# Issuing a small transfer from GpSimd instead of ScalarE, more unread products, and a second PSUM bank in the third segment's end

## The chip, the cores and the metric

The kernel runs on 1 core of one Trainium2 chip. The metric is the time of one execution on the device in microseconds (us). The kernel before has a median of 779.33 us over 3 runs (775.82 to 816.84).

## The reference, cut to what matters

The output is a gated mix of two layers over the same 2048 x 448 input `u`: a long convolution (S4D) and an attention with a memory of the earlier segments (infini-attention, 16 heads of width 28, 4 segments of 512 rows).

```python
# the convolution: a kernel K of 2048 taps for each of 448 channels
P = exp((A * dt)[:, :, None] * pos)              # 448 x 256 states x 2048
K = 2 * einsum("dn,dnl->dl", C, P).real
y = irfft(rfft(K, 4096) * rfft(u.T, 4096))[:, :2048].T + u * D_skip
# the attention, for each segment s in turn
p      = softmax(qs @ ks.T * scale + mask)       # 512 x 512 for each head
a_dot  = p @ vs
a_mem  = (phi(qs) @ M) / (phi(qs) @ z + 1e-6)
o      = g * a_mem + (1 - g) * a_dot             # g = sigmoid(beta), one for each head
M, z   = M + phi(ks).T @ vs, z + sum(phi(ks))
a      = concat(o) @ wo
# the mix, gated for each row
out    = gate * y + (1 - gate) * a
```

## The kernel before, in words

**Two halves.** The first half, up to about 421 us of the span, builds the taps K, the projections q, k and v, the transform of `u` and the segments' memories; nothing in it is touched. The function `second_half` (L1310) writes out the rest: the softmax attention, the second half of the convolution, and the outputs.

**Units and rounds.** The attention is cut into 16 units; unit i is segment `s = i // 4` and group of heads `hg = i % 4` (4 heads). Each unit has 6 rounds r. A round issues one `pair` (L1339): products of scores into the PSUM tile `ps_w` (`weigh`, L1069), which ScalarE turns by exp into `PT`, and products into `ps_mx` (`maxima`, L1021), for the row maxima of unit i+2, which VectorE reduces to `mx`. `peak` (L1335) is a piece of the maxima of unit i+1. GpSimd zeroes the upper triangle of `PT` (`affine_select`, L1099) and issues the small transfers of the maxima (`qu<-mn`, L1062). The products of `PT` with V go to `ps_pv` (`values`, L1106) in the next unit's first three rounds; ScalarE copies the result to `pvs`. Row 28 of each head's 32 rows in `pvs` is the softmax denominator, since V has a column of ones. Units 1 to 12 also carry the convolution's pieces (`cv`): products into `ps_c`, copies by ScalarE (`ks`, `bs`), products of VectorE (`pr`).

**Unread products.** Where a round has nothing else for TensorE, `turn_over` (L1347) issues products of the constant `wz` (128 x 512, bf16) into `ps_pv`; nobody reads them. In unit 0 it stands in every round, and twice more ahead of a `peak`.

**The end of a segment.** In round 2 of units 4, 8 and 12 the generator `seg_end(s)` (L1223) is started for segment s = 0, 1, 2 and is then stepped once a round (more often where the table `STEPS`, L1469, says so). It does, a step at a time: `norm` (L1163), which loads the denominators as a 128 x 64 tile `dn` (a transfer from SBUF to SBUF of 32 KB, issued by ScalarE through `k.adma`, L1167), inverts them on VectorE (`inverse`, L1127: reciprocal, hi and lo part), writes them to eight rows `r8` with two transfers issued by ScalarE (`r<-rs`, L1138), and then for each hg spreads them by one product with `sel` into PSUM and scales `pvs` in place (a `scalar_tensor_tensor`, and for s > 0 a `tensor_tensor` that adds the memory's part `am`); `recall` of the next segment (L1146), the same for the memory's denominators `dm`; the skip term (`skip`, `scaled`: `u` times the gate on ScalarE, times D on GpSimd, L1194); and four tiles of the out projection, each with two halves of products (`wo`) into a PSUM tile of tag "m", and `store` (L1196), which adds the skip term on VectorE and sends the tile to `TB`.

**PSUM** in this half: tags "m" and "pv" have one bank each, "mx", "w" and "c" one tile of two banks each. So a second product into "m" waits until VectorE or ScalarE has read the first one. In segment 2's `norm` the odd hg already take half of "c", which the convolution no longer needs.

**Order.** TensorE, ScalarE and VectorE execute in the order in which the code is written (L1481, L1491, L1530). `k.pin` keeps a transfer or an operation at its place on its engine. Transfers from SyncE, `k.dma` and `k.ldma`, take their place on its queue. The functions as they stand before the change:

Of the kernel before, what the change touches and what calls it, by code (L numbers as in the profile page):

```python
# [983 lines left out]
def attend(nc, k, ap):  # L984
# [28 lines left out]

    STEPS = [(b, hp) for b in range(3) for hp in range(2)]
    MSTEPS = [(b, 1 - hp) for b, hp in STEPS]

# [129 lines left out]
    def recall(s):  # L1146

        dn = ap.tile([128, 64], F32, tag="dm", name="dm", bufs=1)
        k.ldma(dn, k.DM[s - 1].rearrange("j h (i f) -> (j h i) f", f=64))
        yield  # L1150
        am[s] = ap.tile([128, 4, SEG], F32, tag="am", name="am", bufs=1)
        k.ldma(am[s], k.AM[:, :, s - 1].rearrange("h p q -> p h q"))
        yield
        v.tensor_scalar(dn, dn, 1e-6, None, ALU.add)
        yield from inverse(dn, 32, r8)
        yield
        for hg in range(4):
            pb = k.ps("m")
            k.mm(pb, k.sel[32:40], r8[32:40, hg], start=True, stop=True)
            v.scalar_tensor_tensor(am[s][:, hg], am[s][:, hg], k.gh[:, hg : hg + 1], pb, ALU.mult, ALU.mult)  # L1160
            yield

    def norm(s):  # L1163

        pvs = pvss[s]
        dn = ap.tile([128, 64], F32, tag="dn", name="dn", bufs=1)
        k.pin(k.adma(  # L1167
            dn,
            pvs.rearrange("(j e) h q -> e j (h q)", e=32)[28].rearrange("j (i f) -> j i f", f=64),
        ))  # L1170
        yield
        yield from inverse(dn, 0, r8)
        yield
        for hg in range(4):
            o = pvs[:, hg]
            pb = k.ps("c")[:, 0] if s == 2 and hg % 2 else k.ps("m")
            k.mm(pb, k.sel[0:8], r8[0:8, hg], start=True, stop=True)
            v.scalar_tensor_tensor(o, o, k.omg[:, hg : hg + 1], pb, ALU.mult, ALU.mult)
            if s > 0:
                v.tensor_tensor(o, o, am[s][:, hg], ALU.add)  # L1180
            yield

    def skip(s, t):

        i = 4 * s + t
        xt = ap.tile([128, D], F32, tag="xt", name="xt", bufs=4)
        k.ldma(xt, k.u[128 * i : 128 * i + 128])
        return xt
# [32 lines left out]
    old = []  # L1221

    def seg_end(s):  # L1223
        xts = [skip(s, t) for t in range(4)]
        sums, memory = norm(s), recall(s + 1)
        recalled = old.pop() if old else iter(())
        old.append(memory)
        next(sums)
        k.scaling = s > 0
        yield  # L1230
        for t in range(4):
            next(recalled, None)
            if t > 1:
                next(sums)
            k.scaling = s > 0 and t < 3
            yield
        for t in range(0, 4, 2):
            scaled(s, t, xts[t])
            scaled(s, t + 1, xts[t + 1])
            k.scaling = t == 2  # L1240
            yield
        next(memory)
        for hg in range(4):
            next(sums)
            k.scaling = hg < 3
            yield
        for t in range(4):
            if t < 3:
                next(memory)
            po = k.ps("m")  # L1250
            out_mm(s, t, po[:, :D], range(2))
            half.append(s)
            yield "po"
            half.pop()
            out_mm(s, t, po[:, :D], range(2, 4))
            store(s, t, po[:, :D], xts[t])
            yield "po"
        if s == 2:
            for _ in memory:
                yield  # L1260
# [49 lines left out]
def second_half(nc, k, ap, tp, fp, fin):  # L1310
# [13 lines left out]
    def step(g):  # L1324
        return next(g, none) is not none
# [9 lines left out]
    def peak(g):  # L1335
        step(g)
        step(g)
# [9 lines left out]
    def turn_over(n):  # L1347
        pt = k.ps("pv")
        for _ in range(n):
            k.mm(pt, wz[:, :128], wz, start=True, stop=True)  # L1350
# [42 lines left out]
    for i in range(16):  # L1393
# [5 lines left out]
        for r in range(6):  # L1399
# [4 lines left out]
            if r < 2:  # L1404
                if r == 1 and k.half:
                    step(ends[0])
                peak(behind)
            if i == 0 and r in (0, 2):
                turn_over(2)
                peak(behind)  # L1410
            k.spread = r in (1, 2)
            if i > 0 and r < 3:
                step(vals)
                busy = True
                if i % 4 == 0:
                    for t in ((0,), (1,), (2, 3))[r]:
                        k.load_v(i // 4, t)
                if r == 2 and i % 4 == 0:
                    ends.append(k.seg_end(i // 4 - 1))
            for _ in range(STEPS.get((i, r), 2 if i == 14 else 1)):  # L1420
                x = next(ends[0], none) if ends else none
                if x is none:
                    ends = ends[1:]
                busy = busy or x == "po"
            k.catch_up()
            if (i, r) in DIVIDE:
                if k.half:
# [38 lines left out]


SKIPS = ((2, 0), (2, 4), (2, 5), (3, 0), (3, 1), (3, 2))
STEPS = {(13, 2): 2, (13, 3): 3, (13, 4): 2, (13, 5): 2}  # L1469
DIVIDE = {(14, 5): 0, (15, 2): 1, (15, 4): 2}  # L1470


# [296 lines left out]
```

## Time and profile before

| what | value |
|---|---|
| median of 3 runs | 779.33 us |
| the profiled execution's own time | 781.14 us |
| its span, first to last instruction | 779.4 us |
| mean granted clock of TensorE | 0.967 |
| TensorE busy, of the span | 682.8 us (88%) |
| TensorE busy between 421 us and the end (358.4 us) | 323.2 us |
| VectorE, ScalarE, GpSimd busy there | 206.4, 146.8, 74.1 us |

The profile page gives one execution. A timeline row has the start in us, the busy time, the engine, the line, the operation, out<-in and a count; `[3.41 <-ACT PT L1485]` says that the engine sat idle for 3.41 us before it, and whose result came last. Nearly every operation of the engines has the line of a helper (L1485, L1531), so groups go by the names of tiles. ACTq and SPq are the queues on which ScalarE and SyncE issue transfers. A row of the table by stretches has the stretch, its length, the busy time (and instructions) of PE, PEld, DVE, ACT and POOL, the granted clock, the DMA engines' busy share and GB/s.

### The profile page before, as it was taken

To read this page: it belongs to the slowest core of one execution; us is meant where nothing else is said; L and a number is where in the kernel's file an instruction comes from. 1 tells how busy PE (TensorE), PEld (TensorE's weight loads), DVE (VectorE), ACT (ScalarE), POOL (GpSimd) and SP (SyncE) were. 2 spreads that over 40 slices of the span, in tenths; PEclk is the share of its full clock that TensorE was granted. 3 is DMA by queue.
4 is the path that set the end of the run, shared out by engine and by line. 5 is a ranking of instruction groups with operands and counts; after the bars stand their busy time and mean duration, and the time that the engine had idled before them with its cause. 6 is when DMAs were issued, how large, how long until landed. Compare 5 with 4: busy or idle time off the path is not lost.

```text
span 779.4 us, 19822 instructions
## 1 busy us (share of the span) xinstructions
PE 682.8 (88%) x8289; PEld 372.7 (48%) x8289; DVE 562.5 (72%) x758; ACT 502.9 (65%) x621; POOL 158.2 (20%) x193
## 2 busy tenths in 40 slices
PE   1685998999988998889999999898999789969997
PEld 1362555666555665557654444343444333434433
DVE  8989679878999788888874345565746575684486
ACT  4877689889999989988986425564535453451220
POOL 5405300110111101110020002242411231141110
PEclk9998999999999999999999989998999899998899
DMA  9428774234563345733357797998767876655786
GB/s 240 130 74 246 235 247 134 64 107 163 162 209 110 108 138 164 226 128 104 129 198 250 286 327 245 324 341 311 256 233 234 277 247 213 227 189 208 175 267 185
DMA packets 91742, 158.00 MB, mean 203 GB/s; under 512 B 22366, under 2 KB 59734, under 8 KB 91654
## 3 DMA queue, kind: packets, MB, share of 16 engines
q1 hardware_dynamic: 85722, 153.55, 60.0%
q10 hardware_dynamic: 5052, 2.33, 1.2%
q8 instruction: 65, 1.06, 0.6%
q0 software_dynamic: 880, 0.87, 0.3%
q14 instruction: 23, 0.19, 0.1%
HBM read 88.51 MB, written 60.24 MB: 191 GB/s over the span
## 4 chain that ended last, share of the span: by engine, by line
PE 54%; ACT 18%; DVE 14%; DMA 7%; issue 5%; SPq 1%; POOL 1%; ACTq 0%; DVEq 0%; POOLq 0%
PE ps_m L1531 22%; PE ps_c L1531 9%; ACT cs L1485 6%; PE ps_w L1531 6%; PE ps_pv L1531 5%; PE ps_mx L1531 5%; PE ps_arg L1531 4%; PE ps_k L1531 4%; ACT EY L1485 2%; DVE pr L1485 2%; DMA ku<-KD 2%; DVE mx L1485 2%; DVE pvs L1485 1%; DMA WD<-wsp 1%; DVE xl L906 1%
## 5 line engine op out<-in xcount | busy, mean ns | idle before, releaser
L1485 DVE TENSOR_REDUCE mx<-ps_mx 128x2 f32<-128x1024 f32 (+3 forms) x128 | 102.5, 822 | 98.7 <-PE ps_mx L1531 95.6
L1485 ACT ACTIVATE PT<-ps_w 128x1024 f32<-128x1024 f32 (+1 forms) x96 | 84.6, 881 | 132.2 <-PE ps_w L1531 120.3
L366 POOL TENSOR_TENSOR EX<-EX,cab 128x1024 f32<-128x1024 f32 x28 | 53.5, 1914 | 288.2 <-ACT EX L1485 266.4
L1531 PE MATMUL ps_w<-qu,ku 32*128 32x512 f32 (+3 forms) x768 | 90.8, 354 | 10.0 <-ACT PT L1485 9.9
L1485 ACT ACTIVATE cs<-ps_arg 128x1024 f32<-128x1024 f32 x97 | 94.5, 1024 | 3.5 <-DVE Y L414 2.4
L1531 PEld LDWEIGHTS ps_w<-qu,ku 32*128 32x128 f32 x768 | 60.2, 194 | 74.1 <-ACT PT L1485 40.1
L1099 POOL TENSOR_SCALAR_AFFINE_SELECT PT<-PT 128x256 f32<-128x256 f32 (+1 forms) x96 | 47.0, 489 | 229.0 <-ACT PT L1485 226.7
L1531 PE MATMUL ps_m<-xh,w 112*128 112x512 f32 x256 | 91.3, 409 | 1.1 <-DMA w<-WD 1.1
L409 DVE TENSOR_TENSOR X<-EX,cs 128x1024 f32<-128x1024 f32 x56 | 69.4, 1239 | 12.7 <-ACT cs L1485 11.8
L1531 PE MATMUL ps_k<-Y,X 128*32 128x64 f32 x3584 | 64.1, 225 | 14.4 <-DVE Y L414 14.4
L1531 PEld LDWEIGHTS ps_k<-Y,X 128*32 128x32 f32 x3584 | 54.9, 113 | 40.3 <-DVE Y L414 23.2
L413 DVE TENSOR_TENSOR Y<-EY,cs 128x1024 f32<-128x1024 f32 x56 | 70.2, 1253 | 0.0
L1485 ACT ACTIVATE cs<-cs 128x1024 f32<-128x1024 f32 x56 | 59.2, 1057 | 1.3
L1531 PEld LDWEIGHTS ps_m<-xh,w 112*128 112x128 f32 x256 | 48.0, 188 | 20.8 <-issue 7.8
L1485 ACT ACTIVATE EY<-ps_arg 128x1024 f32<-128x1024 f32 x52 | 51.3, 1036 | 4.2 <-PE ps_arg L1531 4.0
L1531 PE MATMUL ps_arg<-ct,lh 64*128 64x512 bf16 x224 | 46.0, 384 | 7.1 <-ACT EY L1485 4.8
L1531 PE MATMUL ps_m<-xl,w 112*128 112x512 f32 x128 | 50.3, 393 | 0.0
L1531 PEld LDWEIGHTS <-lh 64*128 64x128 bf16 x392 | 20.1, 94 | 59.0 <-issue 46.7
L1531 PE MATMUL ps_mx<-ku,qu 32*128 32x512 f32 (+3 forms) x256 | 45.2, 384 | 0.3 <-DMA ku<-KD 0.3
L1531 PE MATMUL ps_pv<-PT,V 128*32 128x128 f32 (+3 forms) x512 | 44.0, 441 | 0.0
L1531 PE MATMUL ps_m<-wo,pvs 128*128 128x448 f32 x96 | 42.4, 572 | 1.4 <-ACT mn L1485 1.1
L415 DVE SCALAR_TENSOR_TENSOR Y<-EY,cs 128x512 f32<-128x512 f32 x56 | 40.1, 716 | 3.8 <-ACT cs L1485 2.6
(219 smaller groups left out, 1292.2 us busy)
## 6 DMA issues: line engine op xcount, KB each, us to landing
w<-WD SPq DMA_DIRECT2D x32, 448.0 KB
qu<-QD SPq DMA_DIRECT2D x16, 512.0 KB
ku<-KD SPq DMA_DIRECT2D x16, 512.0 KB
GU<-gs SPq DMA_DIRECT2D x32, 224.0 KB
GK<-gs SPq DMA_DIRECT2D x8, 896.0 KB
gk<-GK SPq DMA_DIRECT2D x16, 448.0 KB
gu<-GU SPq DMA_DIRECT2D x16, 448.0 KB
ks<-ks SPq DMA_DIRECT2D x32, 224.0 KB
```

The costliest lines, as they stand in the source:

```text
L366: nc.gpsimd.tensor_tensor(o, o, cab, ALU.mult)
L409: v.tensor_tensor(X, ex, t[:, :, 0], ALU.mult)
L413: v.tensor_tensor(Y[:, :, :, :32], lo, y[:, :, :, ::-1], ALU.mult)
L415: v.scalar_tensor_tensor(Y[:, 1, :, 32:], ey[:, :, 32:], -1.0, y[:, 1], ALU.mult, ALU.mult)
L906: v.tensor_tensor(xl[:, :, ts_], pv, xh[:, :, ts_], ALU.subtract)
L1099: nc.gpsimd.affine_select(sl, sl, pat, ALU.is_ge, 0.0, base=0, channel_multiplier=-1)
L1485: x = op(*args, **kw)
L1531: tc.keep_in_program_order(nc.tensor.matmul(*args, **kw))
```

## The change

It has four parts. (1) `norm` issues the transfer `dn<-pvs` from GpSimd instead of ScalarE, for all three segments. (2) Unit 0 gets four unread products ahead of the peak of round 0, and four instead of two behind it, six more in all. (3) In the end of segment 2 the skip term's four products move forward to the steps t = 3 and the next, so that the generator has one step less, and `STEPS` gives up its second step in round 2 and its third in round 3 of unit 13: the scalings are then hg 0 in round 2, hg 1 and 2 in round 3, hg 3 in round 4, together with the first half of the first tile. The odd tiles of segment 2's out projection and the odd products of `recall(3)` take half of "c" instead of "m". (4) Two reorderings in the code: the loads of `u` come after the first step of `norm`, and the loads of V's tiles 2 and 3 after the step of the segment's end. On SyncE's queue the second moves nothing.

```diff
--- before.py
+++ after.py
@@ -1155,7 +1155,7 @@
         yield from inverse(dn, 32, r8)
         yield
         for hg in range(4):
-            pb = k.ps("m")
+            pb = k.ps("c")[:, 0] if s == 3 and hg % 2 else k.ps("m")
             k.mm(pb, k.sel[32:40], r8[32:40, hg], start=True, stop=True)
             v.scalar_tensor_tensor(am[s][:, hg], am[s][:, hg], k.gh[:, hg : hg + 1], pb, ALU.mult, ALU.mult)
             yield
@@ -1164,7 +1164,7 @@
 
         pvs = pvss[s]
         dn = ap.tile([128, 64], F32, tag="dn", name="dn", bufs=1)
-        k.pin(k.adma(
+        k.pin(k.pdma(
             dn,
             pvs.rearrange("(j e) h q -> e j (h q)", e=32)[28].rearrange("j (i f) -> j i f", f=64),
         ))
@@ -1221,20 +1221,23 @@
     old = []
 
     def seg_end(s):
-        xts = [skip(s, t) for t in range(4)]
         sums, memory = norm(s), recall(s + 1)
         recalled = old.pop() if old else iter(())
         old.append(memory)
         next(sums)
+        xts = [skip(s, t) for t in range(4)]
         k.scaling = s > 0
         yield
         for t in range(4):
             next(recalled, None)
             if t > 1:
                 next(sums)
+            if s == 2 and t == 3:
+                scaled(s, 0, xts[0])
+                scaled(s, 1, xts[1])
             k.scaling = s > 0 and t < 3
             yield
-        for t in range(0, 4, 2):
+        for t in range(2 if s == 2 else 0, 4, 2):
             scaled(s, t, xts[t])
             scaled(s, t + 1, xts[t + 1])
             k.scaling = t == 2
@@ -1247,7 +1250,7 @@
         for t in range(4):
             if t < 3:
                 next(memory)
-            po = k.ps("m")
+            po = k.ps("c")[:, 0] if s == 2 and t % 2 else k.ps("m")
             out_mm(s, t, po[:, :D], range(2))
             half.append(s)
             yield "po"
@@ -1404,17 +1407,18 @@
             if r < 2:
                 if r == 1 and k.half:
                     step(ends[0])
+                if i + r == 0:
+                    turn_over(4)
                 peak(behind)
             if i == 0 and r in (0, 2):
-                turn_over(2)
+                turn_over(4 - r)
                 peak(behind)
             k.spread = r in (1, 2)
             if i > 0 and r < 3:
                 step(vals)
                 busy = True
-                if i % 4 == 0:
-                    for t in ((0,), (1,), (2, 3))[r]:
-                        k.load_v(i // 4, t)
+                if i % 4 == 0 and r < 2:
+                    k.load_v(i // 4, r)
                 if r == 2 and i % 4 == 0:
                     ends.append(k.seg_end(i // 4 - 1))
             for _ in range(STEPS.get((i, r), 2 if i == 14 else 1)):
@@ -1422,6 +1426,9 @@
                 if x is none:
                     ends = ends[1:]
                 busy = busy or x == "po"
+            if i > 0 and i % 4 == 0 and r == 2:
+                for t in (2, 3):
+                    k.load_v(i // 4, t)
             k.catch_up()
             if (i, r) in DIVIDE:
                 if k.half:
@@ -1466,7 +1473,7 @@
 
 
 SKIPS = ((2, 0), (2, 4), (2, 5), (3, 0), (3, 1), (3, 2))
-STEPS = {(13, 2): 2, (13, 3): 3, (13, 4): 2, (13, 5): 2}
+STEPS = {(13, 3): 2, (13, 4): 2, (13, 5): 2}
 DIVIDE = {(14, 5): 0, (15, 2): 1, (15, 4): 2}
```

The first place is GpSimd in round 2 of unit 4, where the denominators of segment 0 are loaded. The names: `PT` is the exponential, `qu<-mn` the small transfer of the maxima, `dn<-pvs` the moved one. A piece of the difference:

```order
 L1099 AFFINE_SELECT PT<-PT 128x2x128 x2
 L1062 DMA qu<-mn 4x4x128
-L1099 AFFINE_SELECT PT<-PT 128x2x128 x2
+L1099 AFFINE_SELECT PT<-PT 128x2x128
+L1167 DMA dn<-pvs 128x1x64
+L1099 AFFINE_SELECT PT<-PT 128x2x128
 L1099 AFFINE_SELECT PT<-PT 128x2x256 x2
 L1099 AFFINE_SELECT PT<-PT 128x2x128 x2
```

The transfer now stands between two selects on `PT`; the second of them is behind it on GpSimd, the exponential on ScalarE no longer is.

The second place is ScalarE in the same round, before the change. `pvs<-ps_pv` is the copy with the denominators, `PT<-ps_w` the exponentials that TensorE's scores wait for, `mn` and `bs` copies of the maxima and of the convolution:

```order
L1485 ACTIVATE ks<-ps_c 128x896
L1485 ACTIVATE PT<-ps_w 128x2x512
L1485 ACTIVATE pvs<-ps_pv 128x512
L1167 DMA dn<-pvs 128x1x64
L1485 ACTIVATE PT<-ps_w 128x2x512
L1485 ACTIVATE PT<-ps_w 128x2x256 x2
L1485 ACTIVATE bs<-ps_c 128x896
```

After the change the row of the transfer is gone, and the exponential stands directly behind the copy; at the two later segments likewise.

The third place is TensorE in units 13 and 14, at the third segment's out projection. `ps_m<-wo,pvs` are a tile's products (4 for a whole tile, 2 for half of it), `ps_m<-ident,mx` the transposition of the maxima, which takes the same bank "m". Before:

```order
L1531 MATMUL ps_m<-wo,pvs 128x448 x4
L1531 MATMUL ps_w<-qu,ku 128x512 x6
L1531 MATMUL ps_pv<-PT,V 32x512 x4
L1531 MATMUL ps_m<-wo,pvs 128x448 x4
L1531 MATMUL ps_w<-qu,ku 128x512 x6
L1534 MATMUL ps_m<-ident,mx 16x128
L1531 MATMUL ps_pv<-PT,V 32x384 x4
L1531 MATMUL ps_m<-wo,pvs 128x448 x4
```

The same place after the change, where the helpers' lines are 7 higher:

```order
L1538 MATMUL ps_m<-wo,pvs 128x448 x2
L1538 MATMUL ps_c<-wo,pvs 128x448 x2
L1538 MATMUL ps_w<-qu,ku 128x512 x6
L1538 MATMUL ps_pv<-PT,V 32x512 x4
L1538 MATMUL ps_c<-wo,pvs 128x448 x2
L1538 MATMUL ps_m<-wo,pvs 128x448 x2
L1538 MATMUL ps_w<-qu,ku 128x512 x6
L1538 MATMUL ps_m<-wo,pvs 128x448 x2
L1541 MATMUL ps_m<-ident,mx 16x128
L1538 MATMUL ps_pv<-PT,V 32x384 x4
L1538 MATMUL ps_c<-wo,pvs 128x448 x4
```

The tiles now alternate between the two banks and are cut half a tile later against the rounds; the transposition stands directly behind a tile's last products on the same bank.

## The prediction, made before the changed kernel ran

> **What bounds the kernel now.** I read the shares of the page first, then the table by stretches for the second half of the span, where the change lies.
>
> ```profile
> PE 682.8 (88%) x8289; PEld 372.7 (48%) x8289; DVE 562.5 (72%) x758; ACT 502.9 (65%) x621; POOL 158.2 (20%) x193
> ```
> ```profile
> 460.00:465.00 5.00, 4.07 (x35) 1.67 (x38) 2.27 (x3) 0.74 (x1) 0.40 (x1) 0.61 1.02 393
> 470.00:480.00 10.00, 9.49 (x118) 4.10 (x116) 4.31 (x7) 4.70 (x7) 3.10 (x6) 0.93 0.63 221
> 480.00:530.00 50.00, 46.52 (x664) 20.34 (x660) 31.14 (x37) 30.77 (x42) 16.27 (x28) 1.00 0.99 328
> 530.00:536.00 6.00, 2.71 (x28) 1.08 (x30) 2.23 (x4) 1.62 (x2) 1.04 (x2) 0.73 0.98 360
> 536.00:542.00 6.00, 6.00 (x67) 2.38 (x70) 2.91 (x5) 2.57 (x4) 1.04 (x2) 0.70 0.67 251
> 606.00:612.00 6.00, 2.67 (x25) 1.23 (x25) 1.34 (x2) 2.43 (x3) 1.04 (x2) 0.66 0.98 351
> 700.00:706.00 6.00, 4.28 (x22) 2.10 (x23) 5.66 (x9) 0.60 (x1) 0.53 (x2) 0.50 1.02 409
> 730.00:740.00 10.00, 10.00 (x48) 3.50 (x47) 5.08 (x7) 1.78 (x3) 1.27 (x2) 0.79 1.04 242
> ```
>
> TensorE (PE) is busy for 88%, and in an ordinary stretch (480 to 530) for 46.5 of 50 us at clock 1.00. It loses time in five places: unit 0 (460 to 465, clock 0.61), units 4 and 8 (530 and 606: idle for over half of 6 us, and then a low clock), the third segment's scalings (700 to 706, clock 0.50), and the fourth segment's recall (730 to 740, clock 0.79). The change touches all five. The last columns matter too: the DMA engines' share is 0.98 to 1.02 at 460, from 480 to 536 and again at 606 and 700, and falls only where PE has caught up (0.63 at 470, 0.67 at 536).
>
> Why PE stops in units 4 and 8 stands in ScalarE's timeline and the chain that ended last.
>
> ```profile
> 527.39 0.59 ACT L1485 ACTIVATE pvs<-ps_pv 128x512 f32<-128x512 f32 x1
> 531.06 1.11 ACTq L1167 DMA_DIRECT2D dn<-pvs  x1
> 532.22 1.02 ACT L1485 ACTIVATE PT<-ps_w 128x1024 f32<-128x1024 f32 x1 [4.24 <-issue]
> 602.36 0.59 ACT L1485 ACTIVATE pvs<-ps_pv 128x512 f32<-128x512 f32 x1
> 607.63 0.58 ACTq L1167 DMA_DIRECT2D dn<-pvs  x1
> 608.25 1.02 ACT L1485 ACTIVATE PT<-ps_w 128x1024 f32<-128x1024 f32 x1 [5.30 <-DMA gu<-GU]
> 680.91 0.58 ACTq L1167 DMA_DIRECT2D dn<-pvs  x1
> ```
> ```profile
> 523.64 7.34 DMA cb<-in_c_bk
> ...
> 601.23 6.32 DMA gu<-GU
> ```
>
> The copy `pvs` is done at 527.98 (527.39 + 0.59), but the denominators' transfer goes out at 531.06: just when a transfer that has nothing to do with it, `cb`, has landed (523.64 + 7.34 = 530.98). In unit 8 it goes at 607.63, when `gu` has landed (607.55). ScalarE stands at the issue, and the exponential behind it is 4.24 and 5.30 us late. In unit 12 it goes out at 680.91, and nothing behind it is late.
>
> ```profile
> 533.29 0.58 PE L1531 MATMUL ps_w<-qu,ku 32*128 32x256 f32 x2 [3.41 <-ACT PT L1485]
> 538.58 0.79 PE L1531 MATMUL ps_w<-qu,ku 32*128 32x512 f32 x2
> 603.85 1.74 PE L1531 MATMUL ps_c<-pr,cb 64*64 64x448 f32 x16
> 609.33 0.58 PE L1531 MATMUL ps_w<-qu,ku 32*128 32x256 f32 x2 [3.74 <-ACT PT L1485]
> 615.03 0.49 PE L1531 MATMUL ps_w<-qu,ku 32*128 32x512 f32 x2
> ```
>
> PE waits 3.41 and 3.74 us for that exponential, and the stretches behind are the ones of low clock above. So each wait costs twice: the idle time, and some us of halved products.
>
> **The change, part by part. Denominators, unit 4.** One issue of 1.11 us leaves ScalarE, and the wait with it. The exponential then starts when PE's scores are ready, about 529.0 instead of 532.22, PE's pair about 530.1 instead of 533.29: 3.2. The 5.29 us to unit 5's first pair (538.58) are about half products that halve at full clock and half waits for exponentials; I estimate 4.1, so unit 5 starts at 534.2. Gain 4.4; bounds 3.0 (the idle time alone, the clock falls anyway) and 4.6.
>
> **Unit 8.** From the end of `ps_c<-pr,cb` (605.59) to unit 9's first pair (615.03) PE takes 9.44. The 5.70 from 609.33 on become 4.4 in unit 4's ratio (4.1 of 5.29), and without the wait they begin at 605.59: unit 9 at 610.0, gain 5.0 (5.5 if all its products halve). But the next transfers that ScalarE issues may meet the same wait:
>
> ```profile
> 610.11 0.37 SPq L1547 DMA_DIRECT2D BB<-bs  x1
> 616.50 1.25 ACTq L1138 DMA_DIRECT2D r<-rs  x2
> ```
>
> `r<-rs` would now want to go at about 610.5, close behind SyncE's transfers such as `BB`, while DMA is at 0.98; I take 1.0 us back, 4.0 net (bounds 0, a wait as long as those above, and 5.5).
>
> **Unit 12** waits for nothing there: 0.
>
> **Does the transfer come in time from GpSimd?** Its price there I take from the small transfer that GpSimd issues already, and the time it has from the reciprocals that wait for it.
>
> ```profile
> L1062 POOL DMA_DIRECT2D qu<-mn x16: 582/582/627, 450.9 to 720.8; - x16
> DMA to landing us min/median/max: 1.7/4.0/6.5
> ```
> ```profile
> 537.44 0.54 DVE L1485 RECIPROCAL rc<-dn 128x64 f32<-128x64 f32 x1
> 614.56 0.55 DVE L1485 RECIPROCAL rc<-dn 128x64 f32<-128x64 f32 x1
> 688.56 0.55 DVE L1485 RECIPROCAL rc<-dn 128x64 f32<-128x64 f32 x1
> ```
>
> An issue costs GpSimd 0.58 us, three in all, hidden: GpSimd is busy for 1.04 of 6 us at 530 and at 606 (uncovered they would cost 1.7). Behind it stands one select of `PT`, needed by values a round later. That one moves 8 KB where `dn` has 32, so its time is a bound from below as much as a price; I take it as it is. It lands after 4.0 us (1.7 to 6.5): issued at 528.0, at 532.0, at worst 534.5; the reciprocal, 4.4 earlier than now, wants it at about 533. VectorE goes in order, so a late transfer holds the maxima behind the reciprocal; at worst 1.5 us, at the median nothing. I count 0.
>
> The Trainium skill (SBUF — State Buffer, section "SBUF: two separate sides") speaks against this part: a transfer issued from GpSimd needs descriptors that GpSimd can't write while VectorE runs an operation in a two-port mode. No row here shows it: all 16 such transfers landed within 6.5 us beside a busy VectorE. By the rule the landing would be later, which is the slower rival below; by the rows nothing is lost.
>
> **Unit 0.** Six more products of 512 columns.
>
> ```profile
> 460.93 0.34 PE L1531 MATMUL ps_mx<-mk 32*128 32x128 bf16 x8 [1.26 <-DVE mx L1485]
> 466.32 1.46 PE L1531 MATMUL ps_pv<-wz 128*128 128x512 bf16 x3
> 471.68 0.44 PE L1531 MATMUL ps_w<-qu,ku 32*128 32x384 f32 x2
> 472.70 0.82 PE L1531 MATMUL ps_pv<-wz 128*128 128x512 bf16 x3
> ```
>
> The first four fill the idle 1.26 before 460.93; 3 take 0.82 at full clock, 1.46 at half (472 against 466). If the clock then stays up, the 10.75 us to round 3 (471.68) become 7.4, by walking them again with full-clock durations: gain 3.4. If it falls anyway, six products cost 6 x 0.43 = 2.6 less the 1.26 that they fill: loss 1.3. I take the gain, since the one idle spell there is what they fill.
>
> The Trainium skill (TensorE: Matmul & The Clock Gate, Part 1) says the clock falls after an idle window of about 3.4 us. The 3.41, 3.74 and 4.33 us spells agree; 1.26 us at 460.93 does not. By the rule these products could not raise the clock: the second rival.
>
> **A cap.** Units 0 to 4 together give 3.4 + 4.4 = 7.8, but from 460 to 536 transfers fill the DMA engines. What PE needs sooner must also land sooner, and can move forward only into the slack: 0.37 x 10 us at 470 and 0.33 x 6 at 536, together 5.7. I take 5.7; what is late next is then a load (`ku`, `gu`, `cb`), not ScalarE.
>
> **Third segment.**
>
> ```profile
> 696.88 2.93 DVE L1485 TENSOR_TENSOR pvs<-pvs,am 128x512 f32<-128x512 f32 x1
> 697.05 2.21 POOL L1194 TENSOR_TENSOR xt<-xt,dbc 128x448 f32<-128x448 f32 x2
> 701.70 0.69 DVE L1485 TENSOR_TENSOR pvs<-pvs,am 128x512 f32<-128x512 f32 x1
> ```
> ```profile
> 701.72 0.79 PE L1531 MATMUL ps_c<-r,sel 8*128 8x512 f32 x1 [4.33 <-DVE pvs L1485]
> 726.75 0.49 PE L1531 MATMUL ps_m<-r,sel 8*128 8x512 f32 x1 [0.84 <-DVE am L1485]
> 729.71 0.79 PE L1531 MATMUL ps_m<-r,sel 8*128 8x512 f32 x1 [0.84 <-DVE am L1485]
> ```
>
> One addition on VectorE takes 2.93 us beside GpSimd's skip products (697.05 to 699.26), 0.69 alone; the fourth scaling's product waits 4.33 us behind it on the one bank. With the skip products a round earlier the addition ends at 698.1, not 699.8, and the fourth scaling lies behind the next round's scores. Walking the rows on, PE reaches the recall's first wait at 722.7 instead of 725.9 (726.75 − 0.84): 3.2. It includes 0.8 lost where the transposition now waits for VectorE to read the tile ahead of it on "m". The second bank removes the two waits of 0.84 at 726 and 729: 1.7. Together 4.9; low 2.0 (the waits, little else), high 6.2, if the clock of 0.79 behind them also stays up, which no row explains.
>
> The reordered loads of `u` and V I count at nothing: SyncE issues them in the same order as before, and the skip products that need `u` have rounds of scores ahead of them; if one came late, it would be late by its landing, some us, on GpSimd alone.
>
> **Sum.** 5.7 + 4.0 + 4.9 = 14.6; 781.14 − 14.6 = **766.5 us**. That is against the profiled execution, which is 1.8 above the median; against the median it would be 764.7. I keep the one against the execution that the rows come from.
>
> **The rivals.**
> 1. All of it comes: no cap, nothing given back, the clock up at 730. 3.4 + 4.4 + 5.5 + 6.2 = 19.5, 761.6. For: past 536 the DMA share is down to 0.67, so transfers that come a little late are absorbed there. Against: 0.99 over the 50 us before.
> 2. Unit 0's clock falls anyway: 4.4 + 4.0 + 4.9 − 1.3 = 12.0, 769.1. Against: the fall follows a short spell which is now filled.
> 3. The wait moves on: `r<-rs` and the loads meet the full DMA engines, and units 0 to 8 keep only the 2.0 of slack at 536. 2.0 + 4.9 = 6.9, 774.2. For: 0.98 to 1.02 in every stall of PE. Against: `dn` itself waited for one early transfer, not for the engines' share, and no row shows ScalarE waiting so for `r<-rs` before.
> 4. Slower: GpSimd's transfer lands late and VectorE waits at the reciprocals. They come 9.5 and 11.6 us after the copy's end (537.44 − 527.98, 614.56 − 602.95) and 7.6 after the issue at 680.91, so a landing after L costs 3L − 28.7 and takes the gains of units 4 and 8 away; unit 0 and the third segment still give 8.3. It decides from L = 12.3 (37.0 / 3), twice the longest seen; at L = 14 it is 42 − 28.7 − 8.3 = 5.0 slower, 786.
>
> **How the numbers follow.** Forecast 0.42, rivals 0.22, 0.11, 0.21, 0.04. The range, 757 to 777, goes below the first rival set against the median (759.8) by the 2.1 us that the 4.28 us of products at 700 to 706 would save if the clock stayed up there, rounded down, and beyond the third rival by the third segment's low bound (2.0 for 4.9: 777.1); it leaves out the fourth rival and some of either end. The measurement tells about 2%, 15.6 us, from no change: faster means under 763.7, slower over 794.9. Faster: the first rival's 0.22 and 0.12 of the forecast's own spread (763 to 771). Slower: half of the fourth, 0.02. The rest, 0.64, is same.
>
> **What would show it.** Right: no idle before the exponentials of units 4 and 8, clock 1.00 there and in unit 0; reciprocals without a wait for `dn`; an addition of about 0.7 to 1.9 us in the third segment; no 0.84 before the recall's products. Wrong: ScalarE idle ahead of `r<-rs`, a wait of VectorE for `dn` over 1.5 us, a clock of 0.5 at 461 to 471, or PE idle for `ku`, `gu` or `cb` between 480 and 536.

## The result, and the profile after

| | median | runs | ratio to the kernel before | 95% interval |
|---|---|---|---|---|
| before | 781.15 us | 775.82 to 816.84 | | |
| changed | 768.1 us | 766.05 to 771.38 | 0.9846 | 0.9803 to 0.9888 |

The changed kernel is 1.5% faster, 12.0 us of 781.15 by the ratio. Its profiled execution took 768.64 us with a span of 766.6; the one before had 779.4. The 12.8 us between the two spans are what the two traces can account for. Slow executions, among them the profiled ones of e1_dn, e3_unit0 and e4_no6 below (clock 0.50 from about 418 to 500 us), are left out of all comparisons of times.

The same stretches as before the change, in the table by stretches of the changed kernel (columns: stretch, length, busy time and instructions of PE, PEld, DVE, ACT and POOL, granted clock, DMA share, GB/s):

```profile
460.00:465.00 5.00, 4.75 (x49) 2.21 (x48) 2.90 (x4) 1.20 (x2) 0.40 (x1) 1.00 1.02 397
470.00:480.00 10.00, 8.02 (x91) 3.22 (x94) 3.41 (x6) 3.64 (x6) 2.08 (x4) 0.83 0.63 216
530.00:536.00 6.00, 5.53 (x80) 2.06 (x77) 4.31 (x8) 3.10 (x4) 1.81 (x4) 1.00 1.05 378
606.00:612.00 6.00, 5.21 (x59) 1.83 (x58) 5.55 (x9) 1.95 (x3) 1.04 (x2) 1.00 1.05 375
700.00:706.00 6.00, 6.00 (x25) 2.48 (x25) 1.84 (x6) 1.02 (x1) 0.79 (x2) 1.00 0.92 335
```

All the low clocks that stood at these places are gone (0.61, 0.73, 0.66, 0.50 became 1.00). At 530 TensorE is busy for 5.53 us instead of 2.71, at 606 for 5.21 instead of 2.67. A low one stands at 470 (0.83, before 0.93), just behind unit 0.

ScalarE in unit 4 of the changed kernel (start, time, operation; the bracket is the idle time before and what ended it):

```profile
526.92 0.59 ACT L1492 ACTIVATE pvs<-ps_pv 128x512 f32<-128x512 f32 x1
528.70 1.02 ACT L1492 ACTIVATE PT<-ps_w 128x1024 f32<-128x1024 f32 x1 [1.19 <-PE ps_w L1538]
...
534.79 1.84 ACTq L1138 DMA_DIRECT2D r<-rs  x2
```

The exponential no longer stands behind an issue; it waits for TensorE, 1.19 us where it was 4.24. GpSimd's side of it, from the rows of line 1167:

```profile
L1167 POOL DMA_DIRECT2D dn<-pvs x3: 709/709/709, 527.8 to 675.0; - x3
...
  DVE rc L1492: 0.9, 2
DMA to landing us min/median/max: 3.5/6.1/6.5
```

An issue takes GpSimd 0.709 us, not 0.58. The transfer lands after 3.5 to 6.5 us, with a median of 6.1, so later than the 4.0 that I took, but within the range; VectorE waits for it 0.9 us in all, in two of the three places.

TensorE of the changed kernel, the waits near the edits that are new or changed (waits that stood before as they are now, such as one of 1.50 us for `pr` at 680.99, are left out):

```profile
474.49 0.50 PE L1538 MATMUL ps_w<-qu,ku 32*128 32x512 f32 x2 [1.62 <-DMA qu<-mn]
...
529.78 0.39 PE L1538 MATMUL ps_w<-qu,ku 32*128 32x256 f32 x2 [0.37 <-ACT PT L1492]
...
543.18 0.47 PE L1538 MATMUL ps_m<-r,sel 8*128 8x512 f32 x1 [0.70 <-DMA r<-rs]
...
615.00 0.45 PE L1538 MATMUL ps_w<-qu,ku 32*128 32x384 f32 x2 [1.39 <-ACT PT L1492]
...
619.14 0.47 PE L1538 MATMUL ps_m<-r,sel 8*128 8x512 f32 x1 [0.36 <-DMA r<-rs]
...
694.68 0.23 PE L1538 MATMUL ps_mx<-mk 32*128 32x128 bf16 x2 [1.00 <-DVE mx L1492]
696.72 1.77 PE L1538 MATMUL ps_m<-wo,pvs 128*128 128x448 f32 x4 [0.89 <-DVE pvs L1492]
...
710.76 0.28 PE L1541 MATMUL ps_m<-ident,mx 128*16 128x128 f32 x1 [0.83 <-DVE tb L1492]
```

The wait of 3.41 is 0.37. What took its place is smaller, but new: unit 1 waits 1.62 us for the transfer of its maxima, the first scaling of unit 5 waits 0.70 for `r<-rs`, unit 9 waits 1.39 for an exponential, and in the third segment 4.33 + 0.84 + 0.84 became 1.00 + 0.89 + 0.83.

The exponential that is late in unit 9 stands, on ScalarE, behind the two issues of `r<-rs`, the second of which ends at 613.88 (the bracket names VectorE's `mx`, which had come by 613.70):

```profile
608.47 1.02 ACT L1492 ACTIVATE PT<-ps_w 128x1024 f32<-128x1024 f32 x1 [1.54 <-PE ps_w L1538]
611.84 2.04 ACTq L1138 DMA_DIRECT2D r<-rs  x2
613.92 1.02 ACT L1492 ACTIVATE PT<-ps_w 128x1024 f32<-128x1024 f32 x1 [4.43 <-DVE mx L1492]
```

**Where the time came from.** The convolution's products `ps_c<-gk,cf` stand at fixed places in TensorE's order, so their starts cut the second half into stretches that hold the same work in every kernel here. These are the cuts, before and changed:

```profile
458.21 0.50 PE L1531 MATMUL ps_w<-qu,ku 32*128 32x512 f32 x2
524.44 0.98 PE L1531 MATMUL ps_c<-gk,cf 64*64 64x448 f32 x8
550.94 0.98 PE L1531 MATMUL ps_c<-gk,cf 64*64 64x448 f32 x8 [0.26 <-ACT bs L1485]
596.60 0.98 PE L1531 MATMUL ps_c<-gk,cf 64*64 64x448 f32 x8
639.25 0.98 PE L1531 MATMUL ps_c<-gk,cf 64*64 64x448 f32 x8
670.29 0.98 PE L1531 MATMUL ps_c<-gk,cf 64*64 64x448 f32 x8 [0.55 <-ACT bs L1485]
732.76 2.40 PE L1531 MATMUL ps_c<-bt,fc 128*64 128x448 f32 x8
```
```profile
458.40 0.50 PE L1538 MATMUL ps_w<-qu,ku 32*128 32x512 f32 x2
...
523.97 0.98 PE L1538 MATMUL ps_c<-gk,cf 64*64 64x448 f32 x8
547.40 1.77 PE L1538 MATMUL ps_c<-gk,cf 64*64 64x448 f32 x8
594.37 0.98 PE L1538 MATMUL ps_c<-gk,cf 64*64 64x448 f32 x8
633.11 0.98 PE L1538 MATMUL ps_c<-gk,cf 64*64 64x448 f32 x8
664.13 0.98 PE L1538 MATMUL ps_c<-gk,cf 64*64 64x448 f32 x8 [0.55 <-ACT bs L1492]
720.48 1.72 PE L1538 MATMUL ps_c<-bt,fc 128*64 128x448 f32 x8
```

Differences of neighbouring starts, for the kernels of the experiments below too (`dn` says who issues the denominators' transfer, "six" whether unit 0 has its six products, "third" whether the third segment is changed; us). The profiles of e1_dn, e3_unit0 and e4_no6 serve from 500 us on, where their clock is as in the others, so they have no A:

| profile | dn | six | third | A units 0-3 | B unit 4 | C | D units 8-9 | E | F third segment |
|---|---|---|---|---|---|---|---|---|---|
| before | ACT | no | no | 66.2 | 26.5 | 45.7 | 42.7 | 31.0 | 62.5 |
| e2_third | ACT | no | yes | 64.7 | 25.8 | 45.7 | 42.7 | 31.0 | 58.9 |
| e3_unit0 | ACT | yes | no | - | 25.3 | 45.7 | 40.9 | 31.0 | 63.7 |
| e8_skip | ACT | no | order alone | 64.7 | 26.6 | 45.7 | 40.8 | 31.0 | 62.9 |
| e9_bank | ACT | no | bank alone | 66.5 | 25.1 | 45.7 | 41.3 | 31.0 | 58.0 |
| e10_dnact | ACT | yes | yes | 63.6 | 26.7 | 45.7 | 42.4 | 31.0 | 58.1 |
| e1_dn | POOL | no | no | - | 22.2 | 45.7 | 38.1 | 31.0 | 62.0 |
| e4_no6 | POOL | no | yes | - | 21.6 | 45.7 | 41.3 | 31.0 | 58.0 |
| e13_nothird | POOL | yes | no | 63.6 | 26.4 | 45.7 | 37.9 | 31.0 | 60.4 |
| changed | POOL | yes | yes | 65.6 | 23.4 | 47.0 | 38.7 | 31.0 | 56.4 |
| a_again | POOL | yes | yes | 65.4 | 21.5 | 45.7 | 38.1 | 31.0 | 58.0 |
| e6_fill | POOL | yes, and 17 | yes | 63.6 | 22.6 | 45.7 | 40.7 | 31.0 | 54.7 |

C and E hold nothing that was edited, and are 45.7 and 31.0 in every one of them but for one C of 47.0 (a low clock that reaches in from unit 5). So a stretch repeats to 0.1 us where nothing waits and the clock stays up. Where the clock falls it does not: the same code in A gives 63.6 to 65.6, in F 56.4 to 58.9, so one execution tells the size of an edit there only to 2 or 3 us.

### The profile page after: what moved, and what is told of

The parts are those of the page before. It is cut to its first block, busy times and chain, and to the rows that moved or that the text cites. A ratio compares the mean times of both kernels' runs of the same rounds, so it can differ in the third digit from the quotient of the medians.

```text
span 766.6 us, 19838 instructions
## 1 busy us (share of the span) xinstructions
PE 677.8 (88%) x8295; PEld 369.8 (48%) x8295; DVE 560.4 (73%) x758; ACT 502.8 (66%) x621; POOL 160.0 (21%) x196
## 3 DMA queue, kind: packets, MB, share of 16 engines
q10 hardware_dynamic: 4656, 2.23, 1.2%
## 4 chain that ended last, share of the span: by engine, by line
PE 50%; ACT 18%; DVE 13%; DMA 11%; issue 5%; SPq 2%; POOL 1%; ACTq 0%; DVEq 0%; POOLq 0%
PE ps_m L1538 19%; PE ps_c L1538 9%; ACT cs L1492 5%; PE ps_w L1538 5%; PE ps_arg L1538 4%; PE ps_pv L1538 4%; PE ps_mx L1538 4%; PE ps_k L1538 3%; ACT EY L1492 2%; DVE mx L1492 2%; DVE pr L1492 2%; DMA WD<-wsp 2%; DMA rest<-TB 1%; DVE pvs L1492 1%; DMA w<-WD 1%
## 5 line engine op out<-in xcount | busy, mean ns | idle before, releaser
L1538 PE MATMUL ps_w<-qu,ku 32*128 32x512 f32 (+3 forms) x768 | 88.1, 345 | 6.9 <-ACT PT L1492 5.1
L1538 PEld LDWEIGHTS ps_w<-qu,ku 32*128 32x128 f32 x768 | 58.1, 187 | 70.3 <-ACT PT L1492 33.2
L409 DVE TENSOR_TENSOR X<-EX,cs 128x1024 f32<-128x1024 f32 x56 | 70.3, 1255 | 12.8 <-ACT cs L1492 11.8
L1538 PE MATMUL ps_mx<-ku,qu 32*128 32x512 f32 (+3 forms) x256 | 43.4, 371 | 0.0
L1538 PE MATMUL ps_arg<-ce,lh 64*128 64x512 bf16 x168 | 33.1, 399 | 10.8 <-ACT EY L1492 6.6
```

The source lines that it names most:

```text
L409: v.tensor_tensor(X, ex, t[:, :, 0], ALU.mult)
L1538: tc.keep_in_program_order(nc.tensor.matmul(*args, **kw))
```

## The experiments

**Each part alone.** The kernel before with one part of the change each. e1_dn has the transfer:

```diff
-        k.pin(k.adma(
+        k.pin(k.pdma(
             dn,
```

> The kernel before with the denominators' transfer issued by GpSimd and nothing else. The theory (the transfer's issue held ScalarE, and that alone cost units 4 and 8 their 3.41 and 3.74 us and the low clock behind): both waits gone in the profile, units 4 to 9 about 10 us shorter before anything is given back, 5 to 9 us faster in all (ratio 0.989 to 0.994). The rival that the wait only moves on to the transfers r<-rs: 0 to 3 us faster. The rival that GpSimd's transfer lands late: slower, with the reciprocals waiting over 5 us.

e2_third has the third segment's edits:

```diff
-            pb = k.ps("m")
+            pb = k.ps("c")[:, 0] if s == 3 and hg % 2 else k.ps("m")
...
+            if s == 2 and t == 3:
+                scaled(s, 0, xts[0])
+                scaled(s, 1, xts[1])
...
-        for t in range(0, 4, 2):
+        for t in range(2 if s == 2 else 0, 4, 2):
...
-            po = k.ps("m")
+            po = k.ps("c")[:, 0] if s == 2 and t % 2 else k.ps("m")
...
-STEPS = {(13, 2): 2, (13, 3): 3, (13, 4): 2, (13, 5): 2}
+STEPS = {(13, 3): 2, (13, 4): 2, (13, 5): 2}
```

> The kernel before with the third segment's edits alone (skip products a round earlier, one step less, the second bank for the odd tiles and the recall). The theory: 4.33 us of waiting and the two waits of 0.84 go, and with them the clock's falls at 700 and 727: 5 to 8 us faster (ratio 0.990 to 0.994). The step as predicted, which left the clock out: 4.9. The rival that the end is set by the loads of the last tiles: under 2 us.

e3_unit0 has the six unread products:

```diff
+                if i + r == 0:
+                    turn_over(4)
                 peak(behind)
             if i == 0 and r in (0, 2):
-                turn_over(2)
+                turn_over(4 - r)
```

> The kernel before with the six unread products in unit 0 alone. The step as predicted: the clock stays at 1.00 and 3.4 us are gained (ratio 0.9956). The theory after reading the changed kernel's trace: the clock stays up, but unit 1 then waits for the transfer of its maxima (qu<-mn), so at most 1.5 us are left, and the units 4 and 8 are as before. The rival that only long idle spells lower the clock: 1.3 us slower.

| kernel | median | ratio | interval | us gained |
|---|---|---|---|---|
| e1_dn | 779.02 | 0.9965 | 0.9932 to 0.9997 | 2.7 |
| e2_third | 778.16 | 0.9952 | 0.9916 to 0.9988 | 3.7 |
| e3_unit0 | 779.10 | 0.9968 | 0.9937 to 0.9998 | 2.5 |

Each is a gain clear of zero; each is below what the theory gave for it, except unit 0, where it lies between the two theories and neither is excluded. The three add up to 8.9 us of the 12.0. An interval is 2.4 to 2.8 us to either side, so the sum falls short within what the measurement can tell.

In e1_dn's profile both waits are gone, as expected; this is unit 4's:

```profile
561.77 0.39 PE L1531 MATMUL ps_w<-qu,ku 32*128 32x256 f32 x2 [0.36 <-ACT PT L1485]
```

There the stretches B and D are 4.3 and 4.6 us shorter than before, with nothing else changed. The median gains less: the compared runs lie from 772.14 to 783.59, 11.5 us apart, those of the changed kernel 5.3 (766.05 to 771.38). What takes the gain back in the longer ones, no profile shows. In e2_third's profile the waits of 4.33 and of 2 x 0.84 are gone (0.90, 0.89 and 0.83 are left), but the clock still falls, at 703.5 for 3.4 us and at 727.4 for 6.8; that part of its expectation failed.

**The changed kernel with one part taken back.** First it ran once more as it is, then without the six products (e4_no6), then with the transfer back on ScalarE (e10_dnact).

> The changed kernel once more, for the comparison with the three others: 766 to 771 us, ratio 0.982 to 0.987 to the kernel before.

```diff
-                if i + r == 0:
-                    turn_over(4)
-                turn_over(4 - r)
+                turn_over(2)
```

> The changed kernel without the six unread products in unit 0. The theory (the clock falls after a stretch of 3.41 us in which little of TensorE's array works): the clock falls at 461 to 465 again, for 7 to 10 us, and the kernel is 2 to 4 us slower than the changed one. The rival that unit 1 waits for its maxima in any case: the same within 1 us.

```diff
-        k.pin(k.pdma(
+        k.pin(k.adma(
             dn,
```

> The changed kernel with the denominators' transfer back on ScalarE. The theory that the waits at the issue come back, and with them the clock's falls in units 4 and 8: 5 to 9 us slower than the changed kernel. The rival that this part is worth what it was alone: 2.7 us slower. The rival that other transfers stand in the way there in any case: the same.

e13_nothird has the edits of e1_dn and e3_unit0 together.

> The change without its third segment: the denominators' transfer from GpSimd and the six products. If the parts add up as they measured alone, 5.2 us faster than the kernel before; by what the changed kernel lacked without its transfer (5.7) and its products (1.5), 6 to 8 us, and the falls of the clock at 697 to 707 and 724 to 734 stand in the profile as before.

| kernel | median | ratio | interval |
|---|---|---|---|
| a_again | 770.39 | 0.9879 | 0.9839 to 0.9920 |
| e4_no6 | 771.93 | 0.9893 | 0.9848 to 0.9939 |
| e10_dnact | 776.04 | 0.9946 | 0.9917 to 0.9974 |
| e13_nothird | 776.16 | 0.9952 | 0.9917 to 0.9987 |

The changed kernel itself measured 0.9879 this time and 0.9846 the first; the expectation, 0.982 to 0.987, missed it by a little. Against that the transfer is worth 5.2 us here (0.9946 less 0.9879, of 780.27), within its expected 5 to 9. Compared directly with the runs of a_again it is 5.4 on average, with about 2.5 to either side, so the rival's 2.7 lies at the edge. The wait for ScalarE is back as it was, in TensorE's timeline of e10_dnact, and so are the falls of the clock, 6.8 us each at 529.7 and 604.8:

```profile
530.47 0.58 PE L1538 MATMUL ps_w<-qu,ku 32*128 32x256 f32 x2 [3.74 <-ACT PT L1492]
```

Without the six products it is 1.1 us slower by the ratios, less than the 2 to 4 expected, and the intervals cannot tell it from nothing, nor from the 2 to 4. Its profile does not show whether the clock falls again at 461, as was expected too. e13_nothird gains 3.7 us, where 6 to 8 or 5.2 were expected (its interval reaches from 1.0 to 6.5). In its trace the wait in unit 5 did move on, to the landing of the inverses (`r<-rs`, two transfers issued from 531.33 on, used at 542.34):

```profile
542.34 0.47 PE L1533 MATMUL ps_m<-r,sel 8*128 8x512 f32 x1 [3.19 <-DMA r<-rs]
```

That is the third rival at its place, and it takes all of B there (26.4, as with ScalarE). In the changed kernel the same wait was 0.70 us, in e1_dn 0.53 and in a_again nothing. SyncE's queue has the same order there in all four, so the wait differs from one execution to the next. It does not explain the median: this execution took 771.09 us, and the compared runs lie from 770.53 to 779.47. Of the two falls that were to stand as before, the profile has one of 3.4 us at 693 and one of 6.8 at 717.

**The third segment's two halves.** e8_skip has of the edits of e2_third the order alone, e9_bank the two lines with the second bank alone.

> The kernel before with the earlier skip products and the third segment's shorter order of steps, without the second bank. The theory that VectorE's addition held up by GpSimd's products, and the wait of 4.33 us behind it, is most of this part: 2 to 4 us faster than the kernel before. The rival that the single bank holds the rounds up in any case: 0 to 1.

> The kernel before with the second bank alone, for the third segment's odd tiles and the odd products of the recall. The step as predicted: the two waits of 0.84 us go, 1.7 us faster; with the fall of the clock at 727, 3 us. The rival that the first bank was free in time anyway: 0.

e8_skip is 3.7 us slower than the kernel before (782.35, ratio 1.0047, 1.0016 to 1.0079), where 2 to 4 us faster were expected: the theory falls. e9_bank is not told apart from the kernel before (778.52, 0.9984, 0.9950 to 1.0019), but a gain of up to 3.9 us, and with it the 1.7 of the prediction, is not excluded either; its profiled execution, the fastest of its twelve, has an F of 58.0, as short as with the whole part. Together the two gain 3.7. TensorE's timeline of e8_skip shows what the order alone does:

```profile
698.28 0.23 PE L1534 MATMUL ps_mx<-mk 32*128 32x128 bf16 x2 [1.01 <-DVE mx L1488]
700.32 3.35 PE L1534 MATMUL ps_m<-wo,pvs 128*128 128x448 f32 x4 [0.60 <-DVE pvs L1488]
707.61 1.77 PE L1534 MATMUL ps_m<-wo,pvs 128*128 128x448 f32 x4 [0.83 <-DVE tb L1488]
713.81 1.77 PE L1534 MATMUL ps_m<-wo,pvs 128*128 128x448 f32 x4 [0.83 <-DVE tb L1488]
719.02 0.28 PE L1537 MATMUL ps_m<-ident,mx 128*16 128x128 f32 x1 [0.83 <-DVE tb L1488]
```

The addition on VectorE is short (1.42 us), and the wait of 4.33 is gone. But the tiles now follow each other within a round, and on one bank each waits until VectorE has read the one before: 1.01 + 0.60 + 3 x 0.83, and the 2 x 0.84 of the recall stay. That is 5.8 us in place of 6.0, and the clock is low for 17.1 us there instead of 13.7. So the new order needs the second bank; how much the bank does without it stays open. The wait of 4.33 is also no constant: in the profiles of e9_bank and e13_nothird, with the order as before, it is 2.11 and 2.23 us, since there VectorE's addition met GpSimd's products later (1.12 and 1.11 us, not 2.93).

**What lowers the clock.** e5_small keeps the count and the length of unit 0's unread products and makes them small.

```diff
-            k.mm(pt, wz[:, :128], wz, start=True, stop=True)
+            q = 32 if k.small else 128
+            k.mm(pt[:q], wz[:q, :q], wz[:q], start=True, stop=True)
```

> The changed kernel in which unit 0's unread products use 32 rows and 32 columns of TensorE's array instead of 128 and 128: the same count, and the same 512 columns streamed. If the clock goes by the time that TensorE is busy, nothing changes: clock 1.00 from 461 to 472, the time of the changed kernel. If it goes by how much of the array works, it falls in unit 0 to 0.5 for 3.4 us or more at a time, and the kernel is 1 to 4 us slower than the changed one.

The table by stretches of e5_small:

```profile
457.33:460.75 3.42, 3.17 (x25) 1.51 (x24) 2.42 (x5) 0.66 (x1) 0.00 (x0) 1.00 1.03 412
460.75:464.16 3.41, 2.95 (x33) 1.35 (x32) 2.03 (x4) 1.02 (x1) 0.40 (x1) 1.00 0.98 329
464.16:484.64 20.48, 20.12 (x152) 8.77 (x150) 7.34 (x10) 5.55 (x7) 3.10 (x7) 0.50 0.66 235
```

TensorE was busy for 2.95 of 3.41 us in the second stretch, and at its end the clock fell and stayed at 0.50 for 20.48 us, through the rest of unit 0 and beyond. The kernel took 778.62 us (ratio 0.9986, 0.9953 to 1.0019): all that the change gives is lost, 8 to 11 us against the changed kernel, where 1 to 4 were expected. So the clock does not go by the time that TensorE is busy; how much of its array works explains it. The same can be seen in the kernel before, in two stretches between the clock's steps:

```profile
624.94:628.35 3.41, 2.33 (x34) 0.95 (x33) 3.38 (x6) 3.09 (x4) 2.20 (x4) 1.00 0.51 156
723.93:727.34 3.41, 2.57 (x38) 1.75 (x36) 1.34 (x3) 1.51 (x2) 0.40 (x1) 1.00 0.18 67
```

After the second, with more busy time (2.57), the clock fell; after the first, with 2.33, it did not. The second holds mostly score products on 32 rows and products with V on 32 columns; the first has two groups of the convolution's, on 64 rows and 64 columns.

I put a number on it. In all 14 profiles the steps of the clock lie a whole number of 3.413 us apart. For each such stretch from 421 to 755 us that ran at full clock I summed, over its products, the columns streamed (twice for f32: 448 of them take 0.42 us in `ps_m<-wo,pvs`, where 512 in bf16 take 0.25 to 0.27) times rows x columns of the array / 128². I divided the sum by 8192, the columns of 16 bf16 products, as an estimate of the most that fits: 3 of them took 0.82 us and 5 took 1.25, so one more takes 0.215, and 3.413 / 0.215 is 15.9. After 36 of the 38 stretches below 0.39 the clock fell, after 17 of the 120 from 0.39 to 0.50, and after 1 of the 1067 above 0.50. It is an estimate (some product records are missing), but it sorts nearly every fall. The Trainium skill (TensorE: Matmul & The Clock Gate, Part 1) has a free-running window of 3413 ns, and the traces agree. The same section ties the fall to an idle window, and there they differ: the window of e5_small was busy for 2.95 us.

**Filling the low stretches.** e6_fill adds 17 unread products of the full array to the changed kernel, where its profile had the low stretches; e12_fill2 adds five more.

```diff
+            if i == 1 and r == 0:
+                turn_over(5)
             pair(w, ahead)
...
+            for _ in range(2 if s < 2 and hg == 0 else 0):
+                k.mm(pb, k.wz[:, :128], k.wz, start=True, stop=True)
             k.mm(pb, k.sel[0:8], r8[0:8, hg], start=True, stop=True)
...
+        if m == 15:
+            k.unread(5)
         pt = k.ps("c")
...
+            if s == 2 and t == 0:
+                k.unread(3)
             po = k.ps("c")[:, 0] if s == 2 and t % 2 else k.ps("m")
```

> The changed kernel with 17 more unread products (128 x 128 of the array) where its profile has a low stretch ahead of a fall of the clock: 5 ahead of unit 1, 2 ahead of the first spread product of segments 0 and 1, 5 ahead of unit 12's last products into c, 3 ahead of the third segment's first tile. The theory that the clock goes by how much of the array works in 3.41 us: the falls at 476, 544 and 681 (13.6 us at half clock) go, 3 to 6 us faster than the changed kernel. The rival that only waits count, and the clock falls for reasons of its own: 17 x 0.27 us of products, 1 to 4 us slower where they do not lie in a wait.

> The changed kernel with the 17 further unread products and five more: 3 ahead of the products that wait for VectorE in unit 8 or 9, and 2 ahead of unit 13's round 4. The theory of the clock: the fall at 609.7 that was left goes too, 1 to 3 us faster than with the 17. The rival that what is left is TensorE's own work: the same within 1 us.

| kernel | median | runs | ratio | interval |
|---|---|---|---|---|
| a_again (same chip as e6_fill) | 770.39 | 767.66 to 773.97 | 0.9879 | 0.9839 to 0.9920 |
| e6_fill | 766.63 | 766.09 to 767.52 | 0.9831 | 0.9791 to 0.9871 |
| e12_fill2 | 769.65 | 768.63 to 770.92 | 0.9893 | 0.9857 to 0.9929 |

e6_fill is 3.8 us faster than the changed kernel beside it, as expected, and all its six runs lie within 1.4 us, below the fastest of a_again. Where the changed kernel waited 1.50 us, at 680.99, the timeline of e6_fill has the five products and a wait of 0.32. The changed kernel, then e6_fill:

```profile
680.99 3.26 PE L1538 MATMUL ps_c<-pr,cb 64*64 64x448 f32 x16 [1.50 <-DVE pr L1492]
```
```profile
678.44 1.25 PE L1547 MATMUL ps_pv<-wz 128*128 128x512 bf16 x5
680.01 1.74 PE L1547 MATMUL ps_c<-pr,cb 64*64 64x448 f32 x16 [0.32 <-DVE pr L1501]
```

Of the falls at 476, 544 and 681 none is left; one at 609.7 is new. e12_fill2 removed that one and has one at 717.5 instead; it measured 3 us more than e6_fill, on another chip, and the intervals overlap. That more products help is not shown.

## Why the prediction came out

The time, 768.1, lies 1.6 above the 766.5 on record, and the waits that each part was to remove are gone. The sizes are further off than the sum: one part gave less than forecast, another more in this execution. So the closeness is partly luck, and the second rival's 769.1 is as near; what speaks against that rival is the clock of 1.00 at 460, not the time. The sizes, from the stretches before and in the changed kernel (for F also the means over the table's profiles without and with the part, e6_fill, e8_skip and e9_bank left out):

| term | predicted | measured |
|---|---|---|
| units 0 to 4 (A and B) | 5.7 | 92.7 to 89.0 in the changed kernel, 3.7; to 86.9 in a_again, 5.8 |
| unit 8 (D) | 4.0 | 42.7 to 38.7, 4.0; to 38.1 in a_again, 4.6 |
| third segment (F) | 4.9 | 62.5 to 56.4, 6.1; means 62.2 (four profiles) to 57.9 (five), 4.3 |
| C, and the spans ahead of A and behind F | 0 | 1.3 lost in C, 0.3 gained |
| sum | 14.6 | 12.8 by the spans |

**Unit 4's wait** was read right: it stood at the issue, until an earlier transfer had landed. Why, the prediction did not say, and the trace of the kernel before does. A semaphore instruction of line 1167 stands on ScalarE ahead of each issue:

```profile
L1167 ACTq EVENT_SEMAPHORE  x3: 17/17/17, 531.0 to 680.2; - x3
```

A semaphore is a counter by which a transfer tells that it has landed. The operands in the trace give its number: in unit 4 the instruction waits for semaphore 102, which `dn<-pvs` itself then uses and which `cb` had used last; in unit 8 it is 104, last used by `gu`. In all six profiles with the transfer on ScalarE, the issue comes 0.07 or 0.08 us after that landing, in both units. In the second half the transfers of SyncE and ScalarE draw on the same eight numbers (101 to 107 and 109), and GpSimd's on eight others (111 to 118). So what holds the issue is a semaphore that the program shares between transfers; that a free semaphore on ScalarE would do as well as GpSimd was not tried.

The pair came at 529.78 (predicted 530.1), and the products at 540.92 came at 535.40, 5.5 earlier, of which 0.5 had come from unit 0: 5.0 where I had 4.4. Then 3.3 of the 5.5 went in the same stretch and the next: the 0.70 us for `r<-rs`, and a low clock of 6.8 us behind a stretch that was busy but light (541 to 544). The time went as the third rival said, at its place, and for a smaller sum.

**Unit 0** was mis-sized. The clock stayed up in unit 0, against the second rival, and the 10.75 us to round 3 became 7.15 (461.07 to 468.22). The step that failed is the next one, that these 3.4 us reach the later units: of them 0.7 was left in A (66.23 to 65.57). What is late next is not a load, as the cap had it, but the small transfer of unit 1's maxima (1.62 us of waiting), and behind that wait the clock fell for 3.4 us. The cap, 5.7 for units 0 to 4, lies between the 3.7 and 5.8 of the two executions, but no `ku`, `gu` or `cb` held TensorE there, so it came near by luck. Without the fall, as in e10_dnact and e13_nothird, A is 63.6, 1.1 to 2.9 below the four profiles without the products.

**Unit 8** came out at its number, and the 1.0 taken back for `r<-rs` was spent as the prediction feared: the wait at the issue moved there. ScalarE's queue waits from 608.50 to 611.80 for semaphore 104, which `BB`, issued at 604.91 and landed at 611.77, had used last; with the two issues behind it that makes the idle 4.43 us before the exponential at 613.92, for which TensorE waits 1.39 us at 615.00. The sign "ScalarE idle ahead of `r<-rs`", which was to show the prediction wrong, is therefore there, and so it is in all eight profiles with the transfer on GpSimd (2.2 to 3.4 us), but it costs little. D is 37.9 to 41.3 us in the six of them in the table, 40.8 to 42.7 in the six with ScalarE.

**Third segment.** The addition came down to 1.41 us, within the 0.7 to 1.9 given as a sign. The earlier order, worth 3.2 in the prediction's walk, needs the second bank under the tiles: on one bank it costs time (e8_skip). Whether the two waits of 0.84 are worth their 1.7 by themselves is not shown (e9_bank). The clock at 727, which "no row explains", comes behind a light stretch (723.93 to 727.34).

**The slower rival** did not come: 6.5 us at most from issue to landing (6.8 in e4_no6), 0.9 us of waiting. The Trainium skill's warning (SBUF — State Buffer, "SBUF: two separate sides") that VectorE in a two-port mode keeps GpSimd from writing descriptors shows at most as a median of 6.1 us where `qu<-mn` had 4.0 before. The larger transfer alone could do that, and no run here separates them.

**What stays open**: what makes the landing of `r<-rs` in unit 5 so different (0.70 us of waiting in one execution, 3.19 in another), and whether the extra 3 us that the combined change first showed over its three parts are more than chance. The fourth part of the change, the later loads of `u` and V in the code, stands in none of e1_dn, e2_third, e3_unit0 and e13_nothird and was not tried alone. That it has a share in the gain, or in the closer runs of the changed kernel, is not excluded.

## What to carry to other kernels

An issue of a transfer can hold its engine until an earlier, unrelated transfer with the same semaphore has landed. Look at which landing the issue comes right behind, and at the semaphore that the two share, and put small urgent transfers where no large one has used theirs just before. The wait can move on to the next issue, as it did to `r<-rs`. When a wait of TensorE goes, the gain is not its length: read what the clock does behind it, and keep the array, not only the engine, at work through every wait. An order of steps can cost time on one bank and pay on two (3.7 us slower alone, 3.7 faster with the second bank), so test such edits together and apart.

## What the runs showed of the hardware

- TensorE's clock steps on a grid of 3.413 us. By the estimate above it fell to 0.50 after 36 of the 38 stretches in which less than 0.39 of what the array could do was done, after 17 of 120 from 0.39 to 0.50, and after 1 of 1067 above. Small products (32 x 32 of 128 x 128) kept the engine 86% busy (2.95 of 3.41 us), and the clock still fell, for 20.48 us.
- The same code differs by some microseconds between executions: four runs of the changed kernel had spans of 764.0, 765.5, 766.6 and 769.3 us at mean clocks of 0.986, 0.984, 0.982 and 0.980. The mean clock alone does not tell the span (a_again's profile had 0.964 and 767.5), and that the grid's position makes the difference was not tested.
- A transfer of 32 KB issued by GpSimd took 0.709 us to issue (8 KB: 0.58), and 3.5 to 6.5 us to land (3.2 to 6.8 over eight profiles).
- The issue of `dn<-pvs` on ScalarE came 0.07 or 0.08 us after the landing of the transfer that had last used its semaphore, in units 4 and 8 of all six profiles that have it there.
- VectorE's addition of two SBUF tiles took 0.69 us alone, 1.1 to 1.4 and up to 2.93 us beside GpSimd's product of two SBUF tiles; in the third segment it was 2.93 where it began beside them and 1.12 where it met their end.
